# Weight loads of a fused attention and mixture-of-experts kernel: ScalarE issues them, three units ahead

## The chip, the core and the metric

The kernel runs on one core of a Trainium2 chip. The metric is the device time of the whole program in microseconds. One core has a matrix engine (TensorE, PE in the rows), three engines for elementwise work (VectorE or DVE, ScalarE or ACT, GpSimd or POOL) and SyncE (SP), which here only issues transfers. Each engine runs its own instructions in strict order; a transfer is an instruction on some engine's queue, and its bytes are then moved by 16 DMA engines that all queues share. An order of instructions is fixed when the kernel is built.

## What is computed

```python
def sm_attn(qq, kk, vv):
    s = np.matmul(qq, kk.transpose(0, 1, 3, 2)) / 8
    a = np.exp(s - s.max(-1, keepdims=True))
    return np.matmul(a / (a.sum(-1, keepdims=True) + 1e-9), vv)
packed = sm_attn(p, k, v)                  # 8 x 8 heads, 32 queries, 576 keys, 64 wide
x = sm_attn(q, packed, packed)             # 576 queries on the 32 packed rows
x = x.transpose(0, 2, 1, 3).reshape(4608, 512)
h = x @ w_in                               # 512 -> 2048
g = where(h >= 1, h, where(h <= -1, 0, (h + 1)**2 / 4))
x = g @ w_out                              # 2048 -> 512
e = argmax(x @ w_gate)                     # one of 8 experts
out = softmax(x @ w_gate)[e] * (relu(x @ w1[e]) @ w2[e])   # 512 -> 1024 -> 512
```

## The kernel before, in words

The program has three stages: the packing (`packing`, L376), 192 steps of the first feed-forward layer, and the expert slots. Matrix products that need more than one pass split an operand into a high part (rounded by a cast) and a low part (the rest).

**Packing.** The 64 heads with 32 packed queries make 16 groups of 4 heads (`NG`). For a group, SP loads keys into `kp` (one of three buffers, L400) and values into `vr` (L408, L409); TensorE makes the scores `sc` (L417); VectorE takes their max `nm` (L424, L425); ScalarE takes the exp (L427); TensorE transposes (`tp` L436, `sc` L438), ScalarE copies the transposes (three copies, L439 to L441); TensorE makes the value product (`tp` L451) and ScalarE scales it into `packed` (L452). From group 9 on a group's value product comes in its own turn, and the first hidden steps of the layer behind (L723 to L753: `h`, `rt`, `gh`, `gl`, `y`) run between the groups.

**Weight units.** Meanwhile 16 units of weights are prepared. `load_unit` (L289) moves 1,024 KB from `wcat` into a raw buffer `wr`, issued by SP at L297. `prep_unit` (L300) takes the abs on ScalarE (L312), works on the bits on VectorE (L313 to L316, tile `ca`), casts the result on ScalarE (L317, high part `wo` or `ws`) and subtracts on VectorE (L318, low part). Units 0 to 11 use three raw buffers in turn. Units 12 to 14 use buffers that hold keys until groups 13, 14 and 15 have been transposed, and unit 15 again an ordinary one. Low and high parts of some units go out to memory (`spill`, L321: 1,024 KB each, on SP).

**The order.** SP issues in the order in which the code is written. The orders of TensorE, VectorE, ScalarE and GpSimd are made by a scheduler at build time, from what each instruction needs; the loop over groups gives only the program's order that it starts from. In that loop three things of the weights stand after a group's own work:

```python
for u in <units of group i>:
    prep_unit(u)
    if 0 < u < NU - 2:                      # NU = 12
        load_unit(u + 2)
for u in {NG - 2: (NU,), NG - 1: (NU + 1,), NG: (NU + 2, NU + 3)}.get(i, ()):
    load_unit(u)
```

At the start, `index_tables` (L129) makes small integer tables for a later stage on GpSimd and VectorE, and GpSimd sets two tiles of the packed keys to zero (`pk`, 128 x 2560, L460; `pkf`, 128 x 512, L461).

Of the kernel before, what the change touches and what calls it, by code (L numbers as in the profile page):

```python
# [37 lines left out]
NU = 12  # L38
# [46 lines left out]
def attn_moe_kernel(ctx, tc, qT, kT, vv, pT, wcat, wg, w2cat, out):  # L85
    nc = tc.nc
    ctx.enter_context(tc.manual_schedule(engines={nc.sync.engine}))
    pe, act, dve, pool, sp = nc.tensor, nc.scalar, nc.vector, nc.gpsimd, nc.sync

    def f32(ap):  # L90
        return ap.bitcast(F32)

    const = ctx.enter_context(tc.tile_pool(name="const", bufs=1))
# [35 lines left out]
    def index_tables(pl):  # L129

        NM = NMIN - EARLY
        k = {}
        pi = pl.tile([P, 2], I32, name="pi")
        pool.iota(pi, pattern=[[-1, 2]], base=0, channel_multiplier=1)
        ti = pl.tile([P, 2], I32, name="tail_i")
        dve.tensor_scalar(out=ti, in0=pi, scalar1=-float(NM), scalar2=0.0, op0=ALU.add, op1=ALU.max)
        hi = pl.tile([P, 2, 2], I32, name="half_i")
        dve.tensor_single_scalar(out=hi[:, 0], in_=ti, scalar=1, op=ALU.arith_shift_right)
        dve.tensor_single_scalar(out=hi[:, 1], in_=ti, scalar=1, op=ALU.bitwise_and)  # L140
        for n in ("p", "tail", "kf", "off", "cap"):
            k[n] = pl.tile([P, 2], F32, name="k_" + n)
        hf = pl.tile([P, 2, 2], F32, name="half_f")
        dve.tensor_copy(hf, hi)
        dve.tensor_copy(k["p"], pi)
        dve.tensor_copy(k["kf"], ti)
        dve.tensor_tensor(out=k["kf"], in0=k["p"], in1=k["kf"], op=ALU.subtract)
        dve.tensor_tensor(out=k["kf"], in0=k["kf"], in1=hf[:, 0], op=ALU.add)
        dve.tensor_scalar(out=k["off"], in0=hf[:, 1], scalar1=float(HS), scalar2=None, op0=ALU.mult)
        dve.tensor_scalar(out=k["tail"], in0=k["p"], scalar1=float(NM), scalar2=None, op0=ALU.is_ge)  # L150
        dve.tensor_scalar(out=k["cap"], in0=k["tail"], scalar1=float(SL - HS), scalar2=-float(SL), op0=ALU.mult, op1=ALU.add)
        tri8 = pl.tile([P, E, E], F32, name="tri8")
        pool.memset(tri8, 0.0)
        for e in range(E):
            pool.memset(tri8[:, e, 0:e + 1], 1.0)
        k["tri"] = tri8
        return k

    slot_index = index_tables(const)

    packed = st2.tile([P, 2 * B, D], F32, name="packed")
# [2 lines left out]
    pk = st2.tile([P, 4, 2, 5 * D], F32R, name="pk")  # L165

    pkf = st2.tile([P, 4, 2 * D], F32, name="pkf")
# [113 lines left out]
    def wtile(n, shape, dt, name):  # L281

        return wpool.tile(shape, dt, name=name, tag=n)
# [2 lines left out]
    wraw = {}  # L286
    RAW = ["wo4", "wo5", "wr"] * 4 + ["pw13", "wo7", "pw03", "wr"]

    def load_unit(u):  # L289

        raw = RAW[u]
        if raw == "wr":
            raw = s1.tile([P, 2, 512, 2], I32, name=f"wr{u}", tag="wr", bufs=1)
        else:
            raw = wtile(raw, [P, 2, 512, 2], I32, f"wr{u}")
        sp.dma_start(raw.rearrange("p h a b -> p (h a b)"), wcat[u])  # L297
        wraw[u] = raw

    def prep_unit(u):  # L300

        raw = wraw.pop(u)
        n, m = divmod(u, 4)
        if m < 2:
            w = wstage[2 * n + m] = wtile(f"ws{m}", [P, 2, 2, 512], F32R, f"ws{u}")
        else:
            w = wout[2 * n + m - 2] = wtile(f"wo{2 * n + m - 2}", [P, 2, 2, 512], F32R, f"wo{u}")
        hi, lo = w[:, :, 0, :], w[:, :, 1, :]
        low, high = raw[:, :, :, 0], raw[:, :, :, 1]
        ca = s1.tile([P, 2, 512], I32, name=f"ca{u}", tag="ca", bufs=2)  # L310

        act.activation(f32(ca), f32(high), AF.Abs)  # L312
        dve.tensor_scalar(out=f32(ca), in0=f32(ca), scalar1=EXP_LO, scalar2=EXP_HI, op0=ALU.max, op1=ALU.min)  # L313
        dve.tensor_scalar(out=ca, in0=ca, scalar1=3, scalar2=0x3FFFFFFF, op0=ALU.logical_shift_left, op1=ALU.bitwise_and)
        dve.scalar_tensor_tensor(out=ca, in0=high, scalar=-0x40000000, in1=ca, op0=ALU.bitwise_and, op1=ALU.bitwise_or)
        dve.scalar_tensor_tensor(out=ca, in0=low, scalar=29, in1=ca, op0=ALU.logical_shift_right, op1=ALU.bitwise_or)  # L316
        act.copy(hi, f32(ca))  # L317
        dve.tensor_tensor(out=lo, in0=f32(ca), in1=f32(hi), op=ALU.subtract)  # L318

    def spill(n, g):  # L320
# [55 lines left out]
    def packing():  # L376
        p1_cm = tc.tile_pool(name="st1p", bufs=1, space=PSUM)
        p1 = p1_cm.__enter__()
        if True:
            NG = B * 2  # L380
            d = {i: {} for i in range(NG)}

            kps = []
            for j in range(3):
                kp = wtile(("pw03", "pw13", "wo7")[j], [P, 2 * P + 3 * S], F32, f"kp{j}")
# [3 lines left out]
            def s1_load(i):  # L389
                b, g = divmod(i, 2)  # L390
                s = d[i]
                kp = kps[i % 3]
                s["pr"] = kp[:, :2 * P].rearrange("p (q c) -> p q c", q=2)
                s["kr"] = kp[:, 2 * P:2 * P + 2 * S].rearrange("p (q c) -> p q c", q=2)
                s["a1"] = kp[:, 2 * P + 2 * S:]
                for h in range(2):
                    r = slice(D * h, D * h + D)
                    dst = kp[r, NP * h:NP * h + 6 * D].rearrange("p (q c) -> p q c", q=2)[:, :, :NP]
                    (dve if i < 3 else pool).tensor_copy(dst, pc[i // B][r, 2 * NP * (i % B):2 * NP * (i % B) + 2 * NP].rearrange("p (q c) -> p q c", q=2))
                sp.dma_start(s["kr"], kT[b, 2 * g:2 * g + 2].rearrange("q p s -> p q s"))  # L400
# [10 lines left out]
            def s1_score(i):  # L411
                s = d[i]
                ps = p1.tile([P, 2, 512], F32, name=f"sc{i}", tag="sc")
                for hf in range(2):
                    for q in range(2):
                        r = slice(D * q, D * q + D)
                        pe.matmul(ps[r, hf, :S // 2], lhsT=s["pr"][:, q, r], rhs=s["kr"][:, q, hf * S // 2:(hf + 1) * S // 2], start=True, stop=True)  # L417
                s["sc"] = ps
# [24 lines left out]
            def s1_av(i):  # L443
                s = d[i]
                ps = s["ps"][:, :D]
                for c in range(5):
                    w = min(P, S - c * P)
                    t = s["tA"][:, c * P:(c + 1) * P] if c < 3 else s["tB"][:w, (c - 3) * P:(c - 2) * P]
                    for j in range(4):
                        r = slice(NP * j, NP * j + NP)  # L450
                        pe.matmul(ps[r, :], lhsT=t[:, r], rhs=s["vr"][:w, c, D * j:D * j + D], start=(c == 0), stop=(c == 4))  # L451
                act.activation(packed[:, i, :], ps, AF.Copy, scale=s["rs"])  # L452
                d[i] = None
# [3 lines left out]
                pc.append(work.tile([P, 512], F32, name=f"pc{i}", tag="yr", bufs=4))  # L457
            sp.dma_start(pc[0], pT[:, :512])
            s1_load(0)
            pool.memset(f32(pk), 0.0)  # L460
            pool.memset(pkf, 0.0)  # L461
            load_unit(0)
            s1_load_v(0)
            s1_load(1)
# [8 lines left out]
            def soon(i, fn):  # L473
                early.setdefault(i, []).append(fn)
# [4 lines left out]
            for c, (load, pieces) in enumerate(tile_chains(0, st2)):  # L479
                soon(1 + c, load)  # L480
                for m in range(3):
                    soon(3 + c + m, pieces[m])
            for i in range(NG + 2):
                if i < NG:
                    s1_score(i)
                    s1_exp(i)
                if 0 < i <= STEP0 + 1:
                    s1_av(i - 1)
                if i < NG:
                    s1_tr(i)  # L490
                if i == NG - 1:
                    p1_cm.__exit__(None, None, None)
                    late.append(ctx.enter_context(tc.tile_pool(name="late", bufs=1, space=PSUM)))
                for fn in early.get(i, []):
                    fn()
                if i + 3 < NG:
                    s1_load(i + 3)
                if i + 2 < NG:
                    s1_load_v(i + 2)
                if STEP0 < i < NG:  # L500
                    s1_av(i)
                if i in (NG, NG + 1):
                    late_product(2, i - NG)
                for u in range(-(-NU * i // NG), -(-NU * (i + 1) // NG)) if i < NG else ((NU,), (NU + 1, NU + 2))[i - NG]:
                    prep_unit(u)
                    if 0 < u < NU - 2:
                        load_unit(u + 2)
                    if u % 4 < 2 and u < 8:
                        todo.append((u // 4, u % 4))
                if i >= 5 and todo:  # L510
                    first_product(*todo[0])
                    spill(*todo.pop(0))
                for u in {NG - 2: (NU,), NG - 1: (NU + 1,), NG: (NU + 2, NU + 3)}.get(i, ()):
                    load_unit(u)
                if i >= STEP0:
                    step()

# [312 lines left out]
    raw = [None] * 4  # L830
# [285 lines left out]
```

## Time and profile before

| what | value |
|---|---|
| time, three runs | 1266.10, 1267.85 and 1269.37 us (median 1267.85) |
| the profiled execution: its time / its span | 1265.53 / 1263.7 us |
| busy over the span, TensorE / VectorE / ScalarE / GpSimd | 1197.3 / 943.2 / 734.9 / 320.7 us |
| TensorE's share of the span | 95% |
| moved by transfers | 128.18 MB |

The profile is of one execution. Times in it count from the start of its span. The rows that matter are shown below; each starts with a time or a window, and in a timeline row the second number is the duration, `xN` the number of like instructions that the row joins, and a bracket the idle time of the engine before it and what ended that. `SPq` and `ACTq` are the queues on which SP and ScalarE issue transfers.

### The profile page before, as it was taken

The page shows a single profiled execution, that of the slowest core. Times are in us where ns is not written, and L with a number is a line of the kernel's source. Part 1 is how long each engine was busy: PE and PEld are TensorE (multiplying, and loading weights), DVE is VectorE, ACT ScalarE, POOL GpSimd, SP SyncE. Part 2 cuts the span into 40 slices and gives each one's busy share as a digit, 9 for nine tenths or more (in the row PEclk, how much of TensorE's full clock was granted, in tenths as well). Part 3 has the DMA queues.
Part 4 walks back from the last instruction along what each step waited for, and adds up shares of the span by engine and source line. Part 5 has one row for each costly group of instructions (what it writes and reads, how often), then busy time and mean ns, then how long its engine had stood idle before and what let it go on. Part 6 is the DMA issues. An engine that isn't in the chain of part 4 may idle for free. (4 is left out here: it accounts for less than half of the span.)

```text
span 1263.7 us, 21251 instructions
## 1 busy us (share of the span) xinstructions
PE 1197.3 (95%) x7210; PEld 995.3 (79%) x7210; DVE 943.2 (75%) x2230; ACT 734.9 (58%) x1438; POOL 320.7 (25%) x567
## 2 busy tenths in 40 slices
PE   5799479999999999999999999999999999999997
PEld 2466367788778888778888887778999999999996
DVE  7886586997985967986869769789766666666653
ACT  4675465677665657556466455646555565555553
POOL 3311003722852014741111256321101001010010
PEclk8799689999999999999999999999999999999999
DMA  9996681035212133111151100421211612112150
GB/s 344 306 353 195 213 288 37 28 99 173 72 48 72 48 114 99 53 58 36 67 162 44 37 9 26 159 51 34 84 43 43 192 34 68 34 43 60 34 175 21
DMA packets 70179, 128.18 MB, mean 101 GB/s; under 512 B 10281, under 2 KB 46633, under 8 KB 66864
## 3 DMA queue, kind: packets, MB, share of 16 engines
q1 hardware_dynamic: 56464, 97.33, 24.0%
q0 software_dynamic: 5840, 18.95, 4.1%
q10 hardware_dynamic: 7760, 10.49, 2.8%
q8 instruction: 59, 0.97, 0.3%
q14 instruction: 56, 0.46, 0.1%
HBM read 162.31 MB, written 31.77 MB: 154 GB/s over the span
## 5 line engine op out<-in xcount | busy, mean ns | idle before, releaser
L723 PE MATMUL h<-ah,pw 128*128 128x256 f32 (+1 forms) x1024 | 245.6, 304 | 13.8 <-DVE rt L747 10.2
L874 DVE TENSOR_TENSOR sw<-raw,sw 128x1024 fp32r<-128x1024 f32 (+1 forms) x152 | 179.8, 1202 | 78.9 <-ACT sw L872 78.8
L890 PEld LDWEIGHTS gh<-gx,sw 128*128 128x128 f32 x1728 | 227.2, 191 | 12.9
L728 PE MATMUL y<-wo,gh 128*128 128x512 f32 x576 | 230.5, 400 | 2.0 <-ACT gh L752 2.0
L890 PE MATMUL gh<-gx,sw 128*128 128x256 f32 x1728 | 230.7, 283 | 0.0
L729 PE MATMUL y<-wo,gh 128*128 128x512 f32 x576 | 228.3, 396 | 0.0
L552 DVE CUSTOM_DVE_ANT_0 jk<-yr,wgb 128x512 bf16<-128x512 f32 x288 | 214.2, 744 | 5.1 <-ACT yr L780 3.0
L723 PEld LDWEIGHTS h<-ah,pw 128*128 128x128 f32 x1024 | 177.3, 191 | 38.9 <-DVE rt L747 14.4
L730 PE MATMUL y<-wo,gl 128*128 128x512 f32 x576 | 188.9, 401 | 2.2 <-POOL gl L753 2.1
L872 ACT CAST sw<-raw 128x1024 fp32r<-128x1024 f32 (+1 forms) x160 | 156.3, 1004 | 59.0 <-PE gy L730 54.1
L745 ACT ACTIVATE rt<-h,half 128x320 f32<-128x320 f32 (+1 forms) x192 | 111.3, 581 | 93.5 <-PE h L723 78.8
L752 ACT CAST gh<-rt 128x512 fp32r<-128x512 f32 (+2 forms) x192 | 98.1, 512 | 102.9 <-DVE rt L747 67.6
L723 PE MATMUL h<-al,pw 128*128 128x256 f32 (+1 forms) x512 | 153.4, 300 | 0.0
L747 DVE SCALAR_TENSOR_TENSOR rt<-h,rt 128x320 f32<-128x320 f32 (+1 forms) x192 | 105.4, 550 | 44.0 <-ACT rt L746 41.7
L730 PEld LDWEIGHTS y<-wo,gl 128*128 128x128 f32 x576 | 105.0, 188 | 31.4 <-POOL gl L753 5.3
L728 PEld LDWEIGHTS y<-wo,gh 128*128 128x128 f32 x576 | 108.9, 189 | 25.3 <-ACT gh L752 3.0
L913 POOL DMA_INDIRECT out<-go,xm x37 | 36.5, 985 | 358.5 <-ACT go L912 301.0
L729 PEld LDWEIGHTS y<-wo,gh 128*128 128x128 f32 x576 | 109.2, 189 | 18.5
L894 ACT ACTIVATE ggh<-gh 128x256 fp32r<-128x256 f32 x144 | 55.3, 384 | 108.7 <-PE gh L890 100.3
L729 PE MATMUL gy<-sw,ggh 128*128 128x512 f32 x288 | 113.9, 395 | 0.0
L728 PE MATMUL gy<-sw,ggh 128*128 128x512 f32 x288 | 113.8, 395 | 0.0
L723 PEld LDWEIGHTS h<-al,pw 128*128 128x128 f32 x512 | 98.2, 192 | 7.5 <-issue 1.0
(220 smaller groups left out, 1753.2 us busy)
## 6 DMA issues: line engine op xcount, KB each, us to landing
raw<-in_w2cat SPq DMA_DIRECT2D x76, 1024.0 KB
ws<-wsd SPq DMA_DIRECT2D x48, 512.0 KB
wr<-in_wcat SPq DMA_DIRECT2D x16, 1024.0 KB
kp<-in_kT SPq DMA_DIRECT2D x16, 576.0 KB
xb<-xs SPq DMA_DIRECT2D x72, 128.0 KB
vr<-in_vv SPq DMA_DIRECT2D x16, 512.0 KB
wsd<-ws SPq DMA_DIRECT2D x8, 1024.0 KB
qr<-in_qT ACTq DMA_DIRECT2D x16, 320.0 KB
```

The lines of the kernel that those rows point to most:

```text
L552: dve.tensor_tensor_reduce(out=junk, in0=rows[j][:, :DM], in1=wgb[0][:, e, :], scale=1.0, scalar=0.0, op0=ALU.mult, op1=ALU.add, accum_out ...
L723: pe.matmul(ps[:, col0:col0 + n], lhsT=w[:, g, part, c], rhs=x[:, g, col0:col0 + n], start=(n_mm == 0), stop=(n_mm == 5))
L728: pe.matmul(y, lhsT=gh, rhs=wh, start=first, stop=False)
L729: pe.matmul(y, lhsT=gh, rhs=wl, start=False, stop=False)
L730: pe.matmul(y, lhsT=gl, rhs=wh, start=False, stop=last)
L745: act.activation(v, ps[:, :W], AF.Relu, bias=half, scale=0.5)
L747: dve.scalar_tensor_tensor(out=v, in0=ps[:, :W], scalar=1.0, in1=v, op0=ALU.max, op1=ALU.min)
L752: act.copy(gh[:, :n], vk[:, :n])
L872: act.copy(w[:, n, 0], r)
L874: (pool if sid == 0 and i else dve).tensor_tensor(out=w[:, n, 1], in0=r, in1=f32(w[:, n, 0]), op=ALU.subtract)
L890: pe.matmul(ps[:, :SL], lhsT=first(sid, 4 * (fc // 4) + k, part)[:, c], rhs=rh[:, k, :], start=(n_mm == 0), stop=(n_mm == 3 * KD - 1))
L894: act.activation(gh[:, :SL], ps[:, :SL], AF.Relu)
```

## The change

Four edits. The loads of units 3 to 15 are issued by ScalarE; the load of unit u + 3 stands in `prep_unit` right behind the cast of unit u, where before that of u + 2 stood behind the whole of unit u. Units 12, 13 and 14 with 15 are loaded in the loop's turns 13, 14 and 15 in place of 14, 15 and 16. The two zero fills are moved from GpSimd to VectorE and stand first there. The call that makes the index tables stands in turn 16 of the loop, in place of ahead of it all.

```diff
-    slot_index = index_tables(const)
+    slot_index = {}
...
-    def load_unit(u):
+    def load_unit(u, eng=sp):
...
-        sp.dma_start(raw.rearrange("p h a b -> p (h a b)"), wcat[u])
+        eng.dma_start(raw.rearrange("p h a b -> p (h a b)"), wcat[u])
...
         act.copy(hi, f32(ca))
+
+        if u + 3 < NU:
+            load_unit(u + 3, act)
         dve.tensor_tensor(out=lo, in0=f32(ca), in1=f32(hi), op=ALU.subtract)
...
+            dve.memset(f32(pk), 0.0)
+            dve.memset(pkf, 0.0)
             kps = []
...
-            pool.memset(f32(pk), 0.0)
-            pool.memset(pkf, 0.0)
...
             for i in range(NG + 2):
+                if i == NG:
+                    slot_index.update(index_tables(const))
...
                     prep_unit(u)
-                    if 0 < u < NU - 2:
-                        load_unit(u + 2)
...
-                for u in {NG - 2: (NU,), NG - 1: (NU + 1,), NG: (NU + 2, NU + 3)}.get(i, ()):
-                    load_unit(u)
+                for u in {NG - 3: (NU,), NG - 2: (NU + 1,), NG - 1: (NU + 2, NU + 3)}.get(i, ()):
+                    load_unit(u, act)
```

The line numbers of the changed kernel are 3 higher from L318 on and 5 higher from L399 on. In the order, a row is a line, an operation and out<-in; the number in a name is that of the group (`nm`, `rs`, `sc`, `kp`, `vr`) or of the unit (`ca`, `wr`, `ws`, `wo`).

VectorE from the max of group 9 to that of group 10, before:

```order
L424 TENSOR_REDUCE nm9_929<-sc9_924 128x1
L313 TENSOR_SCALAR ca8_1078<-ca8_1078 128x1024
L425 TENSOR_SCALAR nm9_929<-nm9_929 128x1
L314 TENSOR_SCALAR ca8_1078<-ca8_1078 128x1024
L315 SCALAR_TENSOR_TENSOR ca8_1078<-wr8_903,ca8_1078 128x1024
L428 TENSOR_SCALAR rs9_932<-rs9_932 128x1
L316 SCALAR_TENSOR_TENSOR ca8_1078<-wr8_903,ca8_1078 128x1024
L429 RECIPROCAL rs9_932<-rs9_932 128x1
L747 SCALAR_TENSOR_TENSOR rt3_1293<-h0_3_1278,rt3_1293 128x512
L424 TENSOR_REDUCE nm10_1013<-sc10_1008 128x1
L318 TENSOR_TENSOR ws8_1077<-ca8_1078,ws8_1077 128x2x512
```

VectorE in the changed kernel, from the second row of unit 9 to the max of group 10 (that of group 9 stands five rows above):

```order
L314 TENSOR_SCALAR ca9_1239<-ca9_1239 128x1024
L321 TENSOR_TENSOR ws8_1048<-ca8_1049,ws8_1048 128x2x512
L315 SCALAR_TENSOR_TENSOR ca9_1239<-wr9_873,ca9_1239 128x1024
L433 TENSOR_SCALAR rs9_903<-rs9_903 128x1
L313 TENSOR_SCALAR ca10_1329<-ca10_1329 128x1024
L316 SCALAR_TENSOR_TENSOR ca9_1239<-wr9_873,ca9_1239 128x1024
L434 RECIPROCAL rs9_903<-rs9_903 128x1
L314 TENSOR_SCALAR ca10_1329<-ca10_1329 128x1024
L315 SCALAR_TENSOR_TENSOR ca10_1329<-wr10_951,ca10_1329 128x1024
L321 TENSOR_TENSOR ws9_1238<-ca9_1239,ws9_1238 128x2x512
L316 SCALAR_TENSOR_TENSOR ca10_1329<-wr10_951,ca10_1329 128x1024
L429 TENSOR_REDUCE nm10_984<-sc10_979 128x1
```

Before, unit 8 alone stands between the two maxima, and unit 9 begins seven rows behind the second of them. In the changed kernel what is left of unit 8 and the whole of units 9 and 10 but the last subtraction of unit 10 stand between them.

ScalarE from the last copy of group 13 to the exp of group 15, before:

```order
L441 COPY vr13_1156<-sc13_1314 64x128
L312 ACTIVATE ca11_1446<-wr11_1276 128x1024
L452 ACTIVATE packed_170<-tp13_1326,rs13_1322 128x64
L312 ACTIVATE ca12_1590<-wr12_1454 128x1024
L317 CAST wo11_1445<-ca11_1446 128x2x512
L427 ACTIVATE kp2_195,rs14_1411<-sc14_1403,nm14_1408 128x576
L439 COPY vr14_1243<-tp14_1415 128x384
L440 COPY vr14_1243<-tp14_1415 128x128
L441 COPY vr14_1243<-sc14_1403 64x128
L452 ACTIVATE packed_170<-tp14_1415,rs14_1411 128x64
L312 ACTIVATE ca13_1653<-wr13_1535 128x1024
L427 ACTIVATE kp0_191,rs15_1497<-sc15_1489,nm15_1494 128x576
```

ScalarE in the changed kernel over the same groups:

```order
L446 COPY vr13_1127<-sc13_1283 64x128
L297 DMA wr12_1337<-in_wcat 128x2048
L457 ACTIVATE packed_139<-tp13_1295,rs13_1291 128x64
L432 ACTIVATE kp2_166,rs14_1382<-sc14_1374,nm14_1379 128x576
L444 COPY vr14_1214<-tp14_1386 128x384
L445 COPY vr14_1214<-tp14_1386 128x128
L312 ACTIVATE ca12_1594<-wr12_1337 128x1024
L446 COPY vr14_1214<-sc14_1374 64x128
L297 DMA wr13_1425<-in_wcat 128x2048
L457 ACTIVATE packed_139<-tp14_1386,rs14_1382 128x64
L312 ACTIVATE ca13_1653<-wr13_1425 128x1024
L432 ACTIVATE kp0_162,rs15_1468<-sc15_1460,nm15_1465 128x576
```

Before, the abs of units 11 and 12 and a cast stand ahead of the exp of group 14, and the abs of unit 13 ahead of that of group 15. In the changed kernel ScalarE issues unit 12 behind the copies of group 13, the exp of group 14 follows with two of its copies, the abs of unit 12 stands ahead of the third, unit 13 is issued behind that, and its abs is ahead of the exp of group 15. From the max of group 15 on the rows of TensorE, VectorE and ScalarE are the same in both kernels.

## Rows read from the trace of the kernel before

**Rows 1.** Windows: length, then busy of each engine, PE's clock, DMA share, GB/s.

```profile
0.00:176.00 176.00, 127.06 (x1182) 86.72 (x1183) 135.18 (x248) 103.11 (x222) 32.05 (x123) 0.85 0.81 281
176.00:1263.70 1087.70, 1070.26 (x6030) 908.62 (x6028) 808.07 (x1983) 631.82 (x1216) 288.68 (x444) 1.00 0.23 72
```

**Rows 2.** The same view between the starts of the groups' maxima.

```profile
69.32:77.77 8.45, 7.83 (x78) 5.18 (x77) 8.45 (x15) 7.29 (x14) 1.76 (x1) 1.00 1.02 392
77.77:87.61 9.84, 9.72 (x83) 7.53 (x82) 8.63 (x15) 7.41 (x15) 0.41 (x2) 1.00 0.94 338
87.61:93.17 5.56, 4.67 (x81) 3.29 (x79) 5.24 (x10) 3.98 (x9) 0.47 (x2) 1.00 0.82 271
93.17:105.02 11.85, 11.85 (x107) 9.12 (x104) 9.21 (x15) 7.55 (x15) 0.80 (x3) 1.00 0.68 252
105.02:114.60 9.58, 9.58 (x58) 6.98 (x57) 9.06 (x17) 6.71 (x13) 2.08 (x4) 1.00 0.41 126
114.60:121.31 6.71, 6.71 (x80) 4.68 (x82) 2.31 (x9) 3.12 (x10) 1.89 (x4) 1.00 0.54 156
```

**Rows 3.** Waits from 0 to 200 us: sum, times, longest.

```profile
ACT ca L312 <- DMA wr<-in_wcat: 18.1, 6, 6.2
```

**Rows 4.** Timeline, 0 to 13 us.

```profile
0.89 0.82 DVE L386 MEMSET kp<- 128x256 f32 x3 [0.89 <-PEq L1100]
...
5.47 2.19 PE L417 MATMUL sc<-kp 128*64 128x288 f32 x8 [5.47 <-DMA kp<-in_kT]
...
6.25 3.26 DVE L137 TENSOR_SCALAR tail_i<-pi 128x2 int32<-128x2 int32 x1 [1.48 <-POOL pi L135]
...
6.49 2.24 POOL L460 MEMSET pk<- 128x2560 f32 x1
...
8.56 1.13 ACT L312 ACTIVATE ca<-wr 128x1024 f32<-128x1024 f32 x1 [6.19 <-DMA wr<-in_wcat]
...
11.71 0.74 ACT L427 ACTIVATE kp<-sc,nm 128x576 f32<-128x576 f32 x1 [2.02 <-DVE nm L425]
```

**Rows 5.** Timeline, 119 to 150 us, ScalarE, SP and the last value product.

```profile
119.13 0.40 ACTq L234 DMA_DIRECT2D qr<-in_qT  x1
...
119.67 0.54 SPq L297 DMA_DIRECT2D wr<-in_wcat  x1
...
124.16 12.67 SPq L297 DMA_DIRECT2D wr<-in_wcat  x2
...
124.48 0.26 ACT L441 COPY vr<-sc 64x128 f32<-64x128 f32 x1
...
127.01 1.12 ACT L312 ACTIVATE ca<-wr 128x1024 f32<-128x1024 f32 x1 [2.27 <-DMA wr<-in_wcat]
...
132.16 1.15 ACT L312 ACTIVATE ca<-wr 128x1024 f32<-128x1024 f32 x1 [3.82 <-DMA wr<-in_wcat]
...
134.12 0.76 ACT L427 ACTIVATE kp<-sc,nm 128x576 f32<-128x576 f32 x1
...
143.15 1.12 ACT L312 ACTIVATE ca<-wr 128x1024 f32<-128x1024 f32 x1 [4.38 <-DMA wr<-in_wcat]
...
145.15 0.74 ACT L427 ACTIVATE kp<-sc,nm 128x576 f32<-128x576 f32 x1 [0.88 <-DVE nm L425]
...
147.88 1.45 PE L451 MATMUL tp<-vr 128*32 128x64 f32 x40 [0.52 <-ACT vr L440]
```

**Rows 6.** Timeline: VectorE's operations of hidden steps and units.

```profile
115.33 0.69 DVE L753 TENSOR_TENSOR gl<-rt,gh 128x512 fp32r<-128x512 f32 x1
...
128.16 0.69 DVE L313 TENSOR_SCALAR ca<-ca 128x1024 f32<-128x1024 f32 x1 [4.58 <-ACT ca L312]
...
129.62 1.22 DVE L315 SCALAR_TENSOR_TENSOR ca<-wr,ca 128x1024 int32<-128x1024 int32 x1
...
134.68 1.22 DVE L318 TENSOR_TENSOR wo<-ca,wo 128x1024 fp32r<-128x1024 f32 x1
```

## The prediction

> **What bounds the kernel now.** I read the busy time by windows first, since the change touches only the packing stage. From 176 us to the end of the span TensorE is busy 1070.26 of 1087.70 us at full clock, so that stretch is a queue of matmuls, and its length is fixed by their sum; in the first 176 us it is busy only 127.06, at a granted clock of 0.85 [rows 1]. From the max of the last group onwards the orders of VectorE, TensorE and ScalarE are the same in both kernels. So if the last group's value product, which ends at 147.88 + 1.45 = 149.33 us [rows 5], comes some us earlier or later, everything behind it does too, and the end with it. I therefore ask for one number: when does the packing of group 15 end.
>
> The packing has three parts. Up to the max (nm) of group 8, at 77.77 us, it is fed by transfers: the DMA engines show a share of 1.02 in the stretch before it [rows 2]. From nm of group 8 to that of group 11, at 105.02 us, VectorE is the tight engine: 8.63 of 9.84, 5.24 of 5.56 and 9.21 of 11.85 us, together 23.08 of 27.25, with TensorE nearly as full [rows 2]. From there to 149.33, which is 44.3 us, TensorE is full for two groups (9.58 of 9.58, 6.71 of 6.71 [rows 2]), and then ScalarE stands still for weights: of the 18.1 us that it waits for weight units at L312 in the first 200 us [rows 3], 2.27, 3.82 and 4.38 us are those of units 11, 12 and 13 [rows 5]. What they hold up is visible: the exp of group 14 at 134.12 stands behind the abs of unit 12 (132.16) and the cast of unit 11, that of group 15 at 145.15 behind the abs of unit 13 (143.15) [rows 5].
>
> **The change, part by part.** *The index tables* move in the text, but their rows stay where they were on VectorE and GpSimd: the scheduler puts them ahead of group 0 in both. Cost nothing.
>
> *The two memsets* go from GpSimd to VectorE. Before, a table step on VectorE lasted 3.26 us, beside the 2.24 us memset of GpSimd that began 0.24 us after it [rows 4]. After, VectorE begins with 3,072 columns. The trace has no such memset; by the three of 256 columns in 0.82 us it is 3072/256 x 0.272 = 3.3 us, from 0.89 on. VectorE is free of the key memsets at about 5.0, the six copies end at 6.3, the tables follow at once, and nm of group 0 can start with the end of the scores, 5.47 + 2.19 = 7.66 us [rows 4]. The exp of group 0 then stands behind the abs of unit 0 (8.56 + 1.13), at 9.7 in place of 11.71: up to 2.0 us earlier [rows 4].
>
> The Trainium skill ("SBUF — State Buffer", Who interferes with whom) says that VectorE in a two-port mode and GpSimd lock each other out for a whole instruction; the 3.26 us row agrees. By that rule taken alone the change would gain up to those 3.3 us at the start, and all the way if nothing behind is fed by transfers.
>
> *The issues on ScalarE.* Thirteen loads leave SP's queue, at 0.54 us each on SP [rows 5], and cost ScalarE about 0.40 each, as its own issue does [rows 5]. About nine fall before nm of group 8, 3.6 us in all, spread between exps. Loading u+3 at the cast of u, where u+2 was loaded after the whole of u, puts about one unit more in flight, 1,024 KB, which at the 392 GB/s of that stretch is 2.7 us ahead of the keys and values of the next groups [rows 2]. Gain at the start and these two losses meet at nm of group 8. Bounds: -2.0 (all of the start is kept) to +3 (nothing of it, and one transfer late). The stretch is fed by transfers whose sum doesn't change, so I take **+0.6**.
>
> *VectorE between nm of group 8 and of group 11.* This is the term that decides. With units landing sooner, the scheduler puts their preparation sooner: in the order after, units 9 and 10 stand whole between the max of group 9 and that of group 10, and unit 11 before that of group 11; before, unit 9 stood behind the max of group 10, and unit 11 behind that of group 13. Counted over the rows from nm of group 8 to nm of group 11, VectorE gets four more L315/L316 (1.22 each), three more L313/L314 (0.69), one more ws and three more wo (1.22 each), and loses one gl (0.69) and one rt (about the same): 4.88 + 2.07 + 4.88 - 1.37 = **10.5 us** [rows 6]. It is an engine in strict order, and the max stands behind all of it, then exp, transposes and the value product. The hiding place is VectorE's idle time there, 27.25 - 23.08 = 4.17 us. Of it 1.21 + 0.32 lie in the first two groups, which wait for TensorE; I leave these 1.53 idle, and fill 2.64. So the stretch grows by 10.46 - 2.64 = **+7.8**; bounds +6.3 (all filled) and +10.5 (none filled).
>
> *From nm of group 11 to the end of group 15.* VectorE now has about 10 us less to do, but TensorE has the same matmuls between the scores of groups 11 and 13, and was full; the copies of group 13 end at 124.48 + 0.26, 19.7 us after nm of group 11 [rows 5]; I take 19.0 (bounds in the sum below). Then ScalarE issues unit 12. Unit 11's abs began 7.3 us after its issue (119.67 to 127.01 [rows 5]); so unit 12's, which now stands between the copies of group 14, begins at 26.3. Before it began 27.1 after nm of group 11, but with group 14's exp behind it; now that exp and two of the three copies are ahead of it. The abs (1.12) and the third copy (0.26) end at 27.7, unit 13 is issued until 28.1, and lands 6.3 later as before (the issue ended at 124.16 + 12.67 = 136.83, the abs began at 143.15 [rows 5]): 34.4. Behind its abs, at 35.6, comes exp 15, whose operands are long there (scores 15 can start at about 29), and from that exp to the end of the value product it was 149.33 - 145.15 = 4.2 us: 39.8, in place of 44.3. That is **-4.5**. Bounds: -2.5, if two spills of 1,024 KB, which SP now sends out beside unit 12 since nothing stands before them any more, cost it 2 us; and -6, if unit 13 lands 1.5 us sooner since it has the lanes alone.
>
> The sum is +0.6 + 7.8 - 4.5 = **+3.9 us**; with all bounds on one side -1.7 and +11.
>
> **Rivals.** *It gains.* VectorE's work up to nm of group 15 is the same in both, so an earlier weight unit fills its idle time and the waits of rows 3 go. For: 10.5 us of waits for units 11 to 13 lie on the chain. Against: units 12 and 13 still wait for the buffers of groups 13 and 14, and only that of unit 11 goes. If nm of group 8 is 2 early and the crowding costs 6.3 because its idle is filled, and the last part gives back all 10.5, it comes to -6.2; I give it -3 to -8. It decides from where the last part gives back more than the 0.6 + 7.8 = 8.4 of the other two. Chance 0.22.
>
> *Only the issue moves.* The Trainium skill ("DMA: Bandwidth & Descriptors", Issuing engines are not separate DMA queues) says that starting transfers on several engines saves only sequencer time. As a mechanism of this kernel: transfers set the pace both before and after, the crowding at groups 9 to 11 is caught up while ScalarE waits for units 12 and 13, and what is left is SP's 13 x 0.54 = 7 us of issue, off the chain: within 2 us. Chance 0.12.
>
> *ScalarE blocks.* A load on ScalarE that has to wait for its buffer, or the abs of unit 12 in the midst of group 14's copies, holds exps behind it. Unit 12 lands with two spills beside it, 3 MB in place of 1; at 392 GB/s that is 8 us in place of 2.7, so the last part loses its 4.5: +8.4, to +14 with the other bounds. Chance 0.06.
>
> The forecast, +1.5 to +10, keeps 0.60.
>
> **Numbers.** The profiled execution took 1265.53 us, 1.8 more than its span, and the median of the three runs is 2.3 above it, at 1267.85. 1267.85 + 3.9 is 1271.75, so **1272**. 0.3%, 3.8 us, is about what a measurement can tell from none. Of the forecast's 0.60 I put 0.42 beyond it, 0.18 within; of the gain 0.19 beyond, 0.03 within; of the third 0.12 within; of the last 0.06 beyond. Faster 0.19, same 0.33, slower 0.48. The range from 1263 (half of the gain case is below) to 1278 (the forecast's +10; the last is above) leaves out about 0.17. The forecast's own is 1269 to 1278.
>
> **What would show it.** Right: nm of group 0 near 8 us; nm of group 8 at 77 to 80; nm of groups 10 and 11 near 103 and 113, VectorE over 90% busy from 80 on with gaps of several us on TensorE between 93 and 104; the wait of unit 11 gone, exp 14 ahead of unit 12, the waits of units 12 and 13 still there; the last value product at about 153; the stretch from there to the end unchanged. Wrong: nm of group 11 at 108 or sooner, which means that VectorE had room that the windows hide or that group 8 came early; or the last part, 44.3 us, shortened by more than 8; or a change of the stretch behind 176 us, which I price at nothing.

## The result, and the profile after

The changed kernel takes 1277.64 us (median of 5 runs, 1274.73 to 1279.11), the kernel before 1268.02 (5 runs). The ratio is 1.0071, with a 95% interval of 1.0053 to 1.0089: about 9 us slower (9.6 by the two medians). The forecast was 1272, slower with a chance of 0.48. The direction and the main mechanism were there, but the size was not: 3.9 us were predicted and 9 came.

The profiled execution has a span of 1276.2 us, 12.5 above that of before. Part of it is the execution, not the kernel: that of before (1265.53 us) was 2.5 below its median, while this one (1277.93) is at its median. So I compare medians for the time, and the two traces only up to the last value product of the packing, where they can be laid beside each other group by group. Starts of the maxima `nm` (L424 before, L429 after) and end of the last value product, each less the time in the trace of before:

| group | 0 | 1 | 2 | 4 | 5 | 8 | 9 | 10 | 11 | 14 | 15 | end of product 15 |
|---|---|---|---|---|---|---|---|---|---|---|---|---|
| after, us late | -2.0 | +0.8 | +4.0 | +7.2 | +7.6 | +6.5 | +6.8 | +14.2 | +12.5 | +11.9 | +13.3 | +10.4 |

Three steps are to be seen: +6.5 up to group 8, +6.0 from there to group 11, -2.1 to the end. The prediction had +0.6, +7.8 and -4.5.

**The start.** The timeline of the changed kernel, VectorE and ScalarE, 1 to 31 us:

```profile
1.37 2.19 DVE L386 MEMSET pk<- 128x2560 f32 x1 [1.37 <-PEq L1103]
...
3.61 0.48 DVE L387 MEMSET pkf<- 128x512 f32 x1
...
6.45 0.94 DVE L137 TENSOR_SCALAR tail_i<-pi 128x2 int32<-128x2 int32 x1
...
8.66 0.76 DVE L429 TENSOR_REDUCE nm<-sc 128x1 f32<-128x576 f32 x1 [0.51 <-PE sc L422]
...
14.08 1.05 ACT L317 CAST ws<-ca 128x1024 fp32r<-128x1024 f32 x1 [1.22 <-DVE ca L316]
...
16.72 0.39 ACTq L297 DMA_DIRECT2D wr<-in_wcat  x1
...
17.16 1.12 ACT L312 ACTIVATE ca<-wr 128x1024 f32<-128x1024 f32 x1 [2.03 <-DMA vr<-in_vv]
...
23.20 1.05 ACT L317 CAST ws<-ca 128x1024 fp32r<-128x1024 f32 x1
...
26.86 0.34 ACTq L297 DMA_DIRECT2D wr<-in_wcat  x1
...
27.24 0.18 ACT L214 COPY pkf<-bt 64x32 f32<-64x32 f32 x1 [2.99 <-DMA vr<-in_vv]
...
27.67 0.23 DVE L213 TENSOR_TENSOR pk<-bt,pk 64x64 fp32r<-64x64 f32 x1 [2.17 <-ACT pk L212]
...
30.27 0.76 DVE L429 TENSOR_REDUCE nm<-sc 128x1 f32<-128x576 f32 x1
```

The fills take 2.19 and 0.48 us, the table step (L137 before, 3.26 us in [rows 4]) shrinks to 0.94, and the max of group 0 comes 2.0 us earlier, as predicted. Then two rows that the kernel before has not. ScalarE ends the cast of unit 0 at 15.13 and does nothing until it has issued unit 3 at 16.72; the row of the abs of unit 1 behind it names what ended its 2.03 us (the issue included): a transfer of values, not one of weights. It ends the cast of unit 1 at 24.25 and does nothing until it has issued unit 4 at 26.86, 2.99 us, and again a transfer of values ended it. Neither load lacked its buffer: that of unit 3 was last read by VectorE's L316 of unit 0, which ended at 14.05, that of unit 4 by L316 of unit 1, at 23.17. In the built program both carry a wait of their own on a completion counter, one of eight (DMAHW0 to DMAHW7) that all transfers of SP and ScalarE use in turn. The order of ScalarE with waits, in the changed kernel:

```
L297 DMA wr3_230<-in_wcat 128x2048 [waits DMAHW0_49,Activation_49]
...
L297 DMA wr4_291<-in_wcat 128x2048 [waits DMAHW5_49,Activation_49]
```

The second wait is for ScalarE's own abs that read the same buffer, long met.

Behind these issues stand a scaling, copies, and the abs of the next unit, and VectorE's max stands behind that unit: at 27.67 VectorE has been idle for 2.17 us. By group 2 the lead of 2.0 is a delay of 4.0.

**The crowded stretch.** Windows of the changed kernel between the maxima of groups 8, 9, 10 and 11 (columns as in [rows 1]):

```profile
84.24:94.43 10.19, 10.19 (x92) 7.83 (x91) 10.19 (x17) 7.05 (x12) 0.59 (x2) 1.00 0.89 310
94.43:107.39 12.96, 7.89 (x71) 5.18 (x71) 12.75 (x17) 7.53 (x12) 2.57 (x4) 0.74 0.80 274
107.39:117.56 10.17, 8.65 (x79) 6.20 (x79) 9.17 (x16) 6.90 (x14) 0.18 (x1) 1.00 0.43 146
```

VectorE is busy 10.19 of 10.19, 12.75 of 12.96 and 9.17 of 10.17 us: 32.11 of 33.32, in place of 23.08 of 27.25 [rows 2]. TensorE, nearly full before (26.24 of 27.25), is busy 7.89 of 12.96 in the middle one. It stands idle from 96.0 to 99.3 us, waiting for the exp of group 9, and runs behind that at a granted clock of 0.50, the lower level of 1.2 GHz, up to 103 us; the mean of the window is 0.74, where it was 1.00. This is the picture that the prediction drew.

**The last part.** SP, ScalarE and the last value product in the changed kernel, 135 to 160 us:

```profile
135.93 1.01 SPq L324 DMA_DIRECT2D wsd<-ws  x2
...
137.01 0.74 ACT L432 ACTIVATE kp<-sc,nm 128x576 f32<-128x576 f32 x1 [1.83 <-DVE nm L430]
...
138.76 0.33 ACTq L297 DMA_DIRECT2D wr<-in_wcat  x1
...
139.12 0.26 ACT L446 COPY vr<-sc 64x128 f32<-64x128 f32 x1
...
148.68 1.12 ACT L312 ACTIVATE ca<-wr 128x1024 f32<-128x1024 f32 x1 [2.72 <-DMA wr<-in_wcat]
...
153.58 1.12 ACT L312 ACTIVATE ca<-wr 128x1024 f32<-128x1024 f32 x1 [2.77 <-DMA wr<-in_wcat]
...
155.58 0.74 ACT L432 ACTIVATE kp<-sc,nm 128x576 f32<-128x576 f32 x1 [0.88 <-DVE nm L430]
...
158.32 1.45 PE L456 MATMUL tp<-vr 128*32 128x64 f32 x40 [0.52 <-ACT vr L445]
```

The exp of group 14 is ahead of unit 12, as the order said, and the wait of unit 11 is gone. But from issue to abs unit 12 took 9.9 us (138.76 to 148.68), where I had taken 7.3 from [rows 5]: two spills of 1,024 KB started 2.8 us ahead of it. From the max of group 11 to the end it is 42.2 us, in place of 44.3.

### The profile page after: what moved, and what is told of

It reads as the page before. It is cut to its first block, busy times and chain, and to the rows that moved or that the text cites. A ratio compares the mean times of both kernels' runs of the same rounds, so it can differ in the third digit from the quotient of the medians.

```text
span 1276.2 us, 21248 instructions
## 1 busy us (share of the span) xinstructions
PE 1200.7 (94%) x7210; PEld 997.3 (78%) x7210; DVE 945.7 (74%) x2232; ACT 734.8 (58%) x1438; POOL 318.2 (25%) x565
```

## The experiments

All were timed in five rounds against the kernel before on the same chip. Theory C is the prediction's: VectorE's max stands in strict order behind weight units that now come sooner. Its rival H came with the trace of after: ScalarE's queue is held by loads that wait for an earlier transfer. The table gives how late the maxima are against the trace of before, as above, and the ratio of times.

| run | group 2 | 5 | 8 | 11 | end of product 15 | ratio (95% interval) |
|---|---|---|---|---|---|---|
| fills alone | -0.4 | +1.4 | -0.4 | -0.1 | +4.1 | 1.0000 (0.9990 to 1.0010) |
| last four alone | 0.0 | 0.0 | -0.1 | -0.1 | -3.1 | 0.9984 (0.9974 to 0.9995) |
| units 3 to 11, ScalarE | +4.5 | +7.8 | +2.7 | +8.7 | +6.4 | 1.0043 (1.0028 to 1.0057) |
| units 3 to 11, SP | +0.4 | +2.4 | +1.0 | +10.0 | +9.4 | 1.0061 (1.0045 to 1.0076) |
| units 9 to 11, SP | +0.5 | +0.5 | +1.8 | +9.1 | +7.3 | 1.0053 (1.0038 to 1.0067) |
| units 3 and 4, ScalarE | +4.4 | +6.4 | +4.4 | +8.4 | +4.1 | 1.0004 (0.9993 to 1.0014) |
| changed, 9 to 11 as before | +4.9 | +8.4 | +6.9 | +16.5 | +9.0 | 1.0082 (1.0067 to 1.0097) |
| changed, fills as before | +4.4 | +7.7 | +1.6 | +7.5 | +3.3 | 1.0026 (1.0016 to 1.0035) |
| last five, ScalarE | +0.1 | +0.1 | -0.1 | +0.3 | -5.7 | 0.9949 (0.9935 to 0.9962) |
| last five, SP | +0.4 | +0.4 | +0.7 | +0.8 | -4.8 | 0.9940 (0.9927 to 0.9952) |
| last six | +0.5 | +0.5 | +0.3 | +0.2 | -1.4 | 0.9971 (0.9960 to 0.9982) |
| last five, fills | -1.4 | -0.3 | -2.0 | -1.6 | -6.2 | 0.9952 (0.9937 to 0.9967) |

### The edits one by one

Fills alone:

```diff
+            dve.memset(f32(pk), 0.0)
+            dve.memset(pkf, 0.0)
             kps = []
...
-            pool.memset(f32(pk), 0.0)
-            pool.memset(pkf, 0.0)
```

> Kernel before with one edit: the two zero fills on VectorE, first there, in place of GpSimd. In the changed kernel the max of group 0 came at 8.66 us in place of 10.68, and by group 2 it was 4.0 late. Theory H (ScalarE's queue is held by a load that waits for an earlier transfer, 2.0 us in front of unit 1's abs and 3.0 us behind unit 1's cast) puts the loss on the issues alone: without them the 2.0 us lead at group 0 stays for some groups, and the time is 0 to 2 us below before (the packing up to group 8 is fed by transfers). Theory C (only the crowding of weight units on VectorE between the maxima costs) expects the same here, since the order of units hardly moves with this edit alone. If the fills themselves delay VectorE's copies of the first queries, the time is above before by 0 to 1 us.

No change: the max of group 0 is 2.8 us earlier, and by group 3 this is gone. The groups from 13 on are 2.7 to 4.2 late (the order of units moves there). The span of this trace is 3.9 us longer too, 1267.6, and yet the medians are the same; why is open, as said in the part on the stretch from the packing to the end.

Last four alone:

```diff
-                for u in {NG - 2: (NU,), NG - 1: (NU + 1,), NG: (NU + 2, NU + 3)}.get(i, ()):
-                    load_unit(u)
+                for u in {NG - 3: (NU,), NG - 2: (NU + 1,), NG - 1: (NU + 2, NU + 3)}.get(i, ()):
+                    load_unit(u, act)
```

> Kernel before with one edit: units 12 to 15 are loaded in turns 13, 14 and 15 by ScalarE; all else, and the order on every engine up to there, as before. The prediction's term for this stretch was -4.5 us (-2.5 to -6): then 1263.5. The changed kernel gave 2.1 us there (12.5 late at the max of group 11, 10.4 late at the exp of group 15), and by that it is -2 us: 1266. If ScalarE's wait for the landing of units 12 and 13 only moves, no change.

A gain of 0.16%, 2.0 us; in the trace 3.1 at the last value product, within the bounds of the prediction's term (-2.5 to -6), short of its -4.5.

Units 3 to 11 by ScalarE, three ahead:

```diff
         act.copy(hi, f32(ca))
+        if u + 3 < NU:
+            load_unit(u + 3, act)
...
-                    if 0 < u < NU - 2:
-                        load_unit(u + 2)
```

> Kernel before with one edit: units 3 to 11 are loaded by ScalarE, each three units ahead at the cast; fills and last four units as before. H: ScalarE is held in front of units 3 and 4 for 1.5 to 3 us each, the max of group 2 is 4 to 6 us late, and the time is 5 to 10 us above before. C: the order has 6.9 us less of VectorE's work ahead of the max of group 8 than before and 3.8 more ahead of that of group 11, so the loss by crowding alone is 0 to 4 us, and the maxima of groups 1 to 3 are not late.

Slower by 0.43%, 5.5 us. The two holds of ScalarE are there again, and group 2 is 4.5 late, as H said. By group 8 it is 2.7; this order has 6.9 us less of VectorE's work up to there.

The same with SP:

```diff
-            load_unit(u + 3, act)
+            load_unit(u + 3, sp)
```

> As the run with units 3 to 11 issued three ahead, but SP issues them, as before. No load stands in ScalarE's queue. H: the maxima of groups 1 and 2 are within 1 us of before, and the time is at most 4 us above before. C: VectorE has 8.2 us more ahead of the max of group 11 than before (the order has that with SP too), of which 4.2 us can hide, so that the time is 4 to 8 us above before. If SP itself is held by a load that waits for its buffer, keys and values come late, and the loss shows at groups 2 to 5.

Slower by 0.61%, 7.7 us, with no weight load on ScalarE's queue. The maxima of groups 1 and 2 are on time, so H is right on what delays them. But the loss is larger, and 9.0 of the 9.4 us come between the maxima of groups 8 and 11. So the loss comes without H, where C puts it.

### Crowding and holding, each by itself

Units 9, 10 and 11 alone one unit earlier, on SP:

```diff
+        if 9 <= u + 3 < 12:
+            load_unit(u + 3, sp)
...
-                    if 0 < u < NU - 2:
+                    if 0 < u < NU - 2 and not 9 <= u + 2 < 12:
                         load_unit(u + 2)
```

> Kernel before with one edit: units 9, 10 and 11 are loaded one unit earlier, by SP as before; units 3 to 8, the last four and the fills stay. The order is that of before up to the max of group 9, and then has 8.8 us more of VectorE's work ahead of the max of group 11. This is the predicted crowding by itself. C: 4.2 us of it can hide in VectorE's idle time, so the max of group 11 is 4.6 to 8.8 us late; 0.5 to 2.3 of that is given back later (as in the two runs with units three ahead), and the time is 3 to 7 us above before. H: nothing is issued by ScalarE, so no loss.

Slower by 0.53%, 6.7 us, and the max of group 11 is 9.1 late. Windows of this run between the maxima of groups 9, 10 and 11:

```profile
89.45:99.84 10.39, 6.57 (x93) 4.93 (x90) 7.74 (x13) 6.09 (x12) 1.06 (x4) 1.00 0.97 310
99.84:114.16 14.32, 12.36 (x99) 9.52 (x100) 14.29 (x21) 10.27 (x19) 0.54 (x2) 1.00 0.33 124
```

Before, the same two took 5.56 and 11.85 us [rows 2]. In the second VectorE is busy 14.29 of 14.32. The granted clock is 1.00 in both, so the lower clock that the changed kernel showed here is not needed for the loss. This run is the clean one: up to the max of group 9 VectorE's order is that of before (1.8 of the 9.1 us stand there already), and three loads that come one unit too soon cost most of what the whole change costs.

Units 3 and 4 alone on ScalarE, the old place left out for them in the same way:

```diff
+        if 3 <= u + 3 < 5:
+            load_unit(u + 3, act)
```

> Kernel before with one edit: units 3 and 4 alone are loaded by ScalarE, three units ahead; all others by SP as before. ScalarE is held before both as in the run with units 3 to 11, so the max of group 2 is about 4.5 us late in both theories. H: that stays to the end, 4 to 6 us above before. C: it is caught up by group 8, since VectorE has nothing more to do up to there than before (-1.1 us in the order), and the time is 0 to 3 us above before (the order has 2.6 us more at group 11).

Group 2 is 4.4 late, by the two holds; in the trace that stays, 4.4 at group 8 and 4.1 at the last product. So C was wrong that it would be caught up by group 8. The span of the trace is 3.3 us longer as well, 1267.0. The median, though, is the same within 0.14%: trace and time don't agree here, and what the two holds cost in time is not shown.

The changed kernel with units 9 to 11 loaded as before:

```diff
-        if u + 3 < NU:
+        if 3 <= u + 3 < 9:
             load_unit(u + 3, act)
...
+                    if 0 < u < NU - 2 and not 3 <= u + 2 < 9:
+                        load_unit(u + 2)
```

> The changed kernel (without the move of the index tables, which leaves the order as it is) with units 9, 10 and 11 loaded as before, by SP and after the whole of the unit two before. The order up to the max of group 9 is that of the changed kernel; from there to the max of group 11 it has 2.3 us more of VectorE's work than before, where the changed kernel had 8.5 more. C: the max of group 9 is about 6.8 us late as in the changed kernel, that of group 11 6 to 8.5 (there 12.5), and the time is 2 to 6 us above before. H: the loss of the changed kernel stays, 8 to 10 us above before.

A miss for C as I had put it: 0.82% slower, no better than the changed kernel. The timeline of this run, ScalarE and VectorE at 102 to 108 us, shows why:

```profile
102.96 1.12 ACT L312 ACTIVATE ca<-wr 128x1024 f32<-128x1024 f32 x1 [1.86 <-DMA wr<-in_wcat]
...
104.12 0.69 DVE L313 TENSOR_SCALAR ca<-ca 128x1024 f32<-128x1024 f32 x1 [3.62 <-ACT ca L312]
...
107.97 0.75 DVE L429 TENSOR_REDUCE nm<-sc 128x1 f32<-128x576 f32 x1
```

The load of unit 9 comes later, but the order still puts that unit ahead of the max of group 10: VectorE waits 3.62 us for its abs, which waits for the landing. From the max of group 9 to that of group 10 it takes 13.08 us with VectorE busy for 8.28; in the changed kernel it was 12.96, with 12.75 busy. There work stood ahead of the max, here waits do in part, and the price is the same. By these two runs it is where the unit stands in VectorE's order that costs, whether it has landed or not.

The changed kernel with the fills on GpSimd as before:

```diff
-            dve.memset(f32(pk), 0.0)
-            dve.memset(pkf, 0.0)
...
+            pool.memset(f32(pk), 0.0)
+            pool.memset(pkf, 0.0)
```

> The changed kernel with the zero fills on GpSimd as before (the call of the index tables too, which leaves the order as it is). Single edits gave +0.4% (loads three ahead by ScalarE), 0 (fills) and -0.2% (last four). If they add, this run is about 3.5 us above before, and the fills, which are nothing alone, cost the changed kernel some 5 us in company: without them the order has 6.9 us less of VectorE's work ahead of the max of group 8, with them none less. So C: the max of group 8 is 2 to 3 us late (6.5 in the changed kernel), that of group 11 about 8.7 (12.5), time +3 to +5. If the time is +8 or more, the fills are innocent, and the last four loads behave otherwise behind late groups.

Only 0.26% slower, 3.3 us: the sum of the single edits. So the fills, which cost nothing alone, cost the changed kernel 5 to 6 us. By the two orders they do that through the place of the units: with them unit 6 stands whole ahead of the max of group 8, where without them it follows, and units 9 and 10 ahead of that of group 10, where without them they follow. The max of group 8 is 6.5 us late with them and 1.6 without. No run has the fills with the other order, so this cause is argued, not shown.

### Versions that beat both

The last four, and unit 11 one unit earlier on SP:

```diff
-                    if 0 < u < NU - 2:
+                    if 0 < u < NU - 2 and not 11 <= u + 2 < 12:
                         load_unit(u + 2)
...
         act.copy(hi, f32(ca))
+        if 11 <= u + 3 < 12:
+            load_unit(u + 3, sp)
```

> A version meant to beat both: the run with the last four units alone, and unit 11 also loaded one unit earlier, by SP. The order then prepares unit 11 between the maxima of groups 12 and 13, where VectorE was busy 2.31 of 6.71 us, in place of between those of groups 13 and 15, where ScalarE and the max of group 14 stood behind its landing. C: 4.4 us of the 6.6 us moved hide there, and the wait of 2.3 us for unit 11 and VectorE's 5 us ahead of the max of group 14 go: 2 to 5 us below the run with the last four alone. If what is moved delays the max of group 13 by more than its waits cost, no gain over that run.

0.51% faster than before. Unit 11 now fills VectorE's idle time between the maxima of groups 12 and 13. The window of this run between them, and rows of the loads of units 15 (119.74) and 12 (126.27), of the spills and of ScalarE:

```profile
114.50:123.53 9.03, 7.76 (x75) 5.11 (x74) 8.86 (x17) 5.78 (x12) 0.72 (x1) 1.00 0.58 191
```

```profile
119.74 0.35 ACTq L297 DMA_DIRECT2D wr<-in_wcat  x1
...
121.76 1.04 SPq L324 DMA_DIRECT2D wsd<-ws  x2
...
126.27 0.35 ACTq L297 DMA_DIRECT2D wr<-in_wcat  x1
...
137.46 1.12 ACT L312 ACTIVATE ca<-wr 128x1024 f32<-128x1024 f32 x1 [2.98 <-DMA wr<-in_wcat]
...
139.47 0.74 ACT L430 ACTIVATE kp<-sc,nm 128x576 f32<-128x576 f32 x1 [0.88 <-DVE nm L428]
```

VectorE is busy 8.86 of 9.03 us there; the max of group 13 is 2.2 late and those of groups 14 and 15 are 1.9 and 4.1 early. Unit 12 takes 11.2 us from issue to abs, behind the two spills that SP sent out at 121.76 and the load of unit 15, which the scheduler put first.

The same with all loads on SP:

```diff
-                    load_unit(u, act)
+                    load_unit(u, sp)
```

> The fastest version so far (unit 11 one unit earlier, last four units one turn earlier) with all its loads on SP. It asks whether the earlier place or ScalarE's queue is what gains. The place alone: within 1 us of that version, 6 us below before. The queue: SP issues units 12 to 15 in its order ahead of two spills and waits there for the buffers of groups 13 to 15, which hold nothing else back before the spills; if the gain needs ScalarE, the time is 2 us or more above that version.

0.60% faster, the fastest of the study, and within the intervals of the run before it. Rows of SP and ScalarE in this run:

```profile
126.80 16.75 SPq L297 DMA_DIRECT2D wr<-in_wcat  x4
...
133.55 1.12 ACT L312 ACTIVATE ca<-wr 128x1024 f32<-128x1024 f32 x1 [2.34 <-DMA wr<-in_wcat]
...
143.60 1.15 SPq L324 DMA_DIRECT2D wsd<-ws  x2
```

Here SP sends the two spills behind the four loads, at 143.60, and unit 12 takes 6.8 us. So the gain is in the earlier place of the loads. ScalarE's queue adds nothing. The Trainium skill ("DMA: Bandwidth & Descriptors", Issuing engines are not separate DMA queues) says that another issuing engine saves only the time to start a transfer; these two runs agree, at 0.9949 and 0.9940. The prediction had this rule as a rival, within 2 us. It failed as that, since the rule speaks of what a queue saves and not of what an engine behind a waiting issue loses; and the run with units 3 to 11 on SP, 7.7 us slower, shows that the earlier place alone is not within 2 us either.

Unit 10 too, against the run with the last five on ScalarE:

```diff
-        if 11 <= u + 3 < 12:
+        if 10 <= u + 3 < 12:
             load_unit(u + 3, sp)
```

> The fastest version so far with unit 10 too loaded one unit earlier by SP. By the order unit 10 is then prepared ahead of the max of group 12, with 0.5 us less of VectorE's work ahead of that of group 11 and 1.4 more ahead of that of group 12; the order from there puts the abs of unit 13 ahead of the exp of group 15. C: VectorE was full between the maxima of groups 11 and 12 (9.06 of 9.58 us), so nothing is won: 0 to 2 us above that version.

0.29% faster than before, 2.8 us above the last five on ScalarE by the ratios, a little worse than expected. The order puts the abs of unit 13 ahead of the exp of group 15, and that exp is at 143.70 where the last five have it at 139.47. The run with all loads on SP has that order too and is the fastest, but there the abs of unit 12 is at 133.55, here at 137.31; so it is the order together with the late landing that costs, as far as the traces show.

The last five on ScalarE, with the two lines of the first run that put the fills on VectorE:

```diff
+            dve.memset(f32(pk), 0.0)
+            dve.memset(pkf, 0.0)
...
-            pool.memset(f32(pk), 0.0)
-            pool.memset(pkf, 0.0)
```

> The fastest version so far with the fills on VectorE. Alone they gave nothing; the order with them has 1.8 us less of VectorE's work ahead of the max of group 8 and 2.4 less ahead of that of group 12. C: within 1.5 us of that version on either side.

0.48% faster, no difference to the run without them.

## Why the prediction was right in direction and short in size

**The start, the step that failed.** The prediction has thirteen loads that "cost ScalarE about 0.40 each", and a term of +0.6 up to group 8 with an upper bound of +3. It measured +6.5. An issue took 0.33 to 0.39 us, as said, but two of them held the engine 1.6 and 2.6 us ahead of it. "ScalarE blocks" was named as a rival, with the wait for a buffer as its cause and the last part as its place; what came was the wait for an earlier transfer's counter, at units 3 and 4. The trace of before does not show it: there SP's loads have waits of the same kind, with only other transfers behind them. The built program of the changed kernel has it. That the stretch is "fed by transfers whose sum doesn't change" was no reason for it to catch up either: the run with units 3 and 4 keeps its 4.4 us in the trace.

The holds alone do not make the +6.5, nor the time. The changed kernel without the fills has them too, 4.4 us at group 2, and is 1.6 late at group 8; its order has 6.9 us less of VectorE's work up to there. It is 3.3 us slower than before, close to the forecast's 3.9; what the 9 us have beyond that came with the fills, which the prediction had booked as a gain of the start.

**Crowding.** Right in place and sign, and shown by itself by the run with units 9 to 11. In the changed kernel it is +6.0, in place of +7.8 and a lower bound of +6.3, just below it: of 4.17 us of idle time VectorE kept 1.21, as little as the 1.53 that I left, and the busy time was 32.1 us, where 23.1 and the counted 10.5 make 33.5. Two readings were not right. In [rows 2] VectorE is not yet the tight engine, with TensorE "nearly as full": TensorE is the fuller one, 26.24 of 27.25 us against 23.08. VectorE became the tight one by the change. And work is not the whole price: the changed kernel with units 9 to 11 as before shows that a unit ahead of the max costs as much when VectorE in part waits for it.

**The last part.** -2.1, in place of -4.5 and an upper bound of -2.5. The order of events was right. Two sizes were off: the copies of group 13 end 21.8 us after the max of group 11 (139.12 + 0.26, less 117.56), not 19.0, and unit 12 took 9.9 us beside the spills, not 7.3 (2.6 more, where the bound had named 2). By these the abs of unit 12 came 31.1 us after the max of group 11, not 26.3. Half of that came back: unit 13 was issued at 148.77, during that abs and not behind it, and took 4.5 us from the end of its issue to its own abs, not 6.3.

**The fills.** Predicted as part of the start, 2.0 us early at group 0: measured. The table step that lasted 3.26 us beside GpSimd's memset took 0.94 without it, which agrees with the lock-out that the prediction cites from the Trainium skill ("SBUF — State Buffer", Who interferes with whom), though VectorE, whose row starts 0.24 us ahead of the memset's, was the one held; but the lead is gone by group 3 even in the run with the fills alone, and so the gain of up to 3.3 us that the prediction drew from it did not come. That the memset of 2,560 columns takes 2.19 us, not the 2.7 of the estimate, changes nothing. Their larger effect, which by the orders is that on the place of the units, was in the rows that I counted but not told apart from the loads.

**Index tables.** Nothing, as predicted: without that edit the order of TensorE, VectorE, ScalarE and SP is row for row the same.

**From the packing to the end.** The prediction let everything behind the last value product move with it and priced a change of that stretch at nothing. Trace against trace this holds within some us: from the end of the product to the end of the span it is 1114.4 us before, 1116.4 in the changed kernel, and 1113.6 to 1117.8 in the twelve runs. In the ratios it holds for the larger shifts: +10.4, +9.4 and +7.3 at the product became +9.0, +7.7 and +6.7, but two of +4.1 became 0 and 0.5. The trace of before is of an execution 2.5 us below its median, and whether its packing or the rest was short, no trace shows. A part of the scatter is the clock: in the trace of the changed kernel TensorE stands idle for 1.83 us up to 253.32, and the window of 250 to 260 us has a mean granted clock of 0.83 and TensorE busy for 8.17 of 10 us, where before had 1.00, the full 2.4 GHz, and 10.00.

The three terms, as measured, make 6.5 + 6.0 - 2.1 = 10.4 at the last value product. That is just inside the upper bound of the sum, +11, since the start went 3.5 beyond its own upper bound and the crowding came out below its value; and the time, 1277.64, is just inside the range that ended at 1278. Not one of the three terms lies within its own bounds, so that the sum and the time lie within theirs is partly luck.

## What to carry to other kernels

Before a load is moved to an engine that computes, ask what the load itself must wait for, its completion counter too, and what stands behind it there; with the same loads on a queue that only issues, the max of group 2 was 0.4 us late in place of 4.5. Where a scheduler sets the order, bringing data sooner also brings its work sooner, ahead of what the chain needs: look at the order around the reduction that everything waits for, and bring forward only what lands in an idle stretch (here unit 11 and the last four, 0.5 to 0.6% faster). An edit that costs nothing alone cost 5 to 6 us beside the others, by the orders through the place it gave the units, so time it in company too.

## What had not been expected of the hardware

A 1,024 KB load took 4.8 and 6.8 us from issue to abs with no other of that size sent out in the 9 us ahead of it (unit 13 of the changed kernel, unit 12 of the last five on SP), 9.9 with two spills of the same size sent out 2.8 us ahead, and 11.2 with another load and two spills 6.5 and 4.5 us ahead. Nothing else here was new: the two idle times of ScalarE are waits of the built program, which the chip only carried out.
